# New order of steps, with spent buffers reused, in a fused local-attention and shift-MLP kernel

## The chip, the cores and the metric

The kernel runs on one core of one Trainium2 chip. The metric is the device time of one execution in microseconds (us), as the median of several runs. Engines are named as in the profile: PE (matmul) with PEld (its weight loads), DVE (VectorE), ACT (ScalarE), POOL (GpSimd) and SP (SyncE, which issues most DMAs). "Span" is the time from the first to the last instruction of the profiled execution.

## The reference

One sequence of 2048 rows and 512 columns, bfloat16. Cut to what is computed:

```python
xn  = layernorm(x)
# A: local dilated attention, 32 heads of 16, window 8, dilation 2
q, k, v = split(xn @ wqkv)                  # 512 x 1536
logits[s, u] = q[s] . k[s - 2u] / 4         # u = 0..7, masked where s - 2u < 0
s_out = (sum over u of softmax(logits)[s, u] * v[s - 2u]) @ wo
# B: two-stage MLP
h  = gelu(layernorm(xn) @ w1)               # 512 x 512
hs = concat(h group 0 moved by +1 row, 1 by -1, 2 by +2, 3 by -2) @ w2
x1 = xn + hs
y  = x1 + gelu(layernorm(x1) @ w3) @ w4     # 512 x 1376, 1376 x 512
out = x + s_out * silu(y)
```

## The kernel before

**Tiles and chunks.** The 2048 rows are 4 chunks of 512, and each chunk is 4 tiles of 128 rows; tile i of 0 to 15 lies in chunk i // 4. Rows of a chunk are dealt out so that tile j of it holds rows j, j + 4, j + 8 and so on, which turns the row shifts of B into another tile, or the same tile one column further.

**The order is a list.** All steps are small functions, and the text `ORDER` at the head of the file is a list of tokens such as `w1.3.4`: step `w1` for tile 3 into PSUM bank 4. The program calls them in that order, so each engine gets its own instructions in the order of the list and waits, in order, for what an instruction needs. Nothing reorders them later. A buffer that is asked for again waits until every instruction on the tile that held it has ended.

**The steps, and the engine of each.** SP: `ldx`, `ldxp`, `ldxc` load x; `ldv`, `ldw1`, `ldqk`, `ldw2`, `ldw3`, `ldw4`, `ldwo` load weights; `xT`, `hTr`, `x1Tr`, `oTr`, `tE` are DMA transposes from SBUF to SBUF; `vl.q.i.h` fetches half h of the shifted v rows of tile i from a DRAM copy of v; `pre` copies x into the output, `so` writes a finished tile. DVE: `st` (statistics of x), `nm0` and `nmv` (normalise), `rp`, `rr`, `nb` (small), `pw.c.u` (the product q * k for chunk c and window place u), `smx`, `sms`, `smn` (softmax), `xa` (adds w2's result), `st3s`, `nm3` (second layernorm), `ya` (adds w4's result), `vp` (v times attention), `sg` (gate times wo's result), `fav` (adds x). ACT: `sq0` (root for the first four tiles), `ev0a`, `eqk`, `ev`, `eh`, `eg`, `eo`, `eoT` (copies or GELUs out of PSUM), `nm`, `ex` (exp), `si` (silu). POOL: constants, `rs` and `r3` (powers), `kh` (halo of k), `sv` (stores v to DRAM), `soa` (adds a finished tile into the output by DMA).

**PE work.** `tr0` transposes the first four tiles on PE; the other chunks are transposed by `xT`. `qk` (8 blocks a chunk), `v`, `w1`, `w2` are blocks of 4 matmuls of 128x128 by 512 columns; `w3` also 4 (11 blocks a chunk), `w4` 11 (one block a tile). `lg` (16 small matmuls that sum the products per head), `ws` (8) and `wo` (16) use 32 columns of the array each, at four positions. `oTp` transposes the last two tiles of attention output. Six PSUM banks, 0 to 5, are named by the last number of a token; two more hold the logits.

**Buffers the change touches.** x of chunk 0 has four buffers `x_t` of its own; chunks 1 to 3 take turns in two chunk buffers, `xc0` and `xc1`. Products `pw` take turns in three buffers, the v rows `vs` in three. `wqk_sb` holds the q and k weights, `hT` the turned h, `xnT0` and `xnT1` the turned normalised x of even and odd chunks.

**Waits on SP.** SP issues its DMAs in list order. Each one counts on one of eight semaphores in turn, and a DMA waits for the one eight places ahead of it to have landed.

Of the kernel before, what the change touches and what calls it, by code (L numbers as in the profile page):

```python
# [28 lines left out]
rs.5 w1.6.4 eqk.1.6 sv.7 pw.0.7 lg.0.3 nm.8 w2.0.1 eh.6 xT.4 pw.0.6 w2.1.3 xa.0 lg.0.7 kh.2
lg.0.6 qk.1.3.4 nb.5 rr.5 nm.11 st3s.0 pre.s.0 qk.1.1.1 nm.10 smx.0 eqk.1.3 w1.7.0 xT.5 eqk.1.1  # L30
qk.1.0.4 eh.7 w2.2.1 hTr.3 eqk.1.0 xa.1 ex.0 w2.3.0 pw.1.2 xT.6 v.8.3 pw.1.0 w1.8.4 ev.8 sms.0
lg.1.0 eh.8 sv.8 lg.1.2 w1.9.3 v.9.2 eh.9 pw.1.3 qk.2.6.4 ev.9 hTr.4 qk.2.4.3 sv.9 smn.0 eqk.2.6
qk.2.0.2 eqk.2.4 st3s.1 tE.0 w1.12.4 eqk.2.0 xa.2 rq.0 v.11.3 vl.s.1.1 xa.3 r3.0 eh.12 st3s.2
lg.1.3 ev.11 w2.6.0 nm3.0 nm3.1 sv.11 st3s.3 w2.7.3 x1Tr.0 xa.6 w2.4.4 rq.1 xa.7 ldwo.s.2 r3.1
w2.5.0 st3s.6 xa.4 w1.11.3 st3s.7 qk.2.3.4 eh.11 st3s.4 qk.2.7.1 eqk.2.3 rq.3 nm3.3 r3.3 nm3.2
qk.2.1.3 eqk.2.7 vp.1 w1.10.4 eqk.2.1 vl.s.2.1 x1Tr.1 qk.2.2.1 eh.10 xa.5 ws.1.3 eqk.2.2 st.14
v.10.4 eo.1 vl.s.4.0 st3s.5 hTr.5 qk.2.5.3 ev.10 rp.7 rq.2 pw.1.5 r3.2 w1.13.1 eqk.2.5 vl.s.0.1
sv.10 v.13.4 nm3.7 eh.13 nm3.6 rs.7 nm3.5 w3.0.9.3 x1Tr.3 nm3.4 pw.1.6 w3.0.0.1 eg.0.9 hTr.6
w3.0.3.0 nb.7 rr.7 eg.0.0 pw.1.1 nm.15 w3.0.10.3 x1Tr.2 nm.14 w3.0.4.1 vp.0 eg.0.10 xT.7
w3.0.7.2 eg.0.4 ev.13 w2.9.3 vl.s.2.0 eg.0.3 sv.13 eg.0.7 lg.1.1 xa.9 w2.10.0 pw.1.4 ws.0.3  # L40
lg.1.5 st3s.9 eo.0 vl.s.3.1 lg.1.4 lg.1.6 w3.1.1.2 pw.2.0 v.14.3 vl.s.4.1 pw.2.1 eg.1.1 oTr.0
w1.15.4 ev.14 pw.1.7 qk.3.5.2 sv.14 eh.15 vp.2 qk.3.0.3 kh.3 eqk.3.5 qk.3.2.4 eqk.3.0 qk.3.4.2
eqk.3.2 xa.10 lg.1.7 eqk.3.4 st3s.10 ws.2.0 w3.1.0.4 smx.1 eo.2 qk.3.3.0 eg.1.0 qk.3.1.2 eqk.3.3
ldw4.s.0 pw.2.2 ex.1 w1.14.4 qk.3.6.0 vl.s.3.0 qk.3.7.3 eh.14 sms.1 lg.2.0 lg.2.2 lg.2.1 w2.11.1
eqk.3.1 w2.8.5 eqk.3.6 xa.11 eqk.3.7 w3.0.8.2 vl.s.5.1 xa.8 w3.0.6.3 hTr.7 vp.3 eg.0.8 w3.0.5.5
eg.0.6 w3.0.1.2 eg.0.5 pw.2.3 ws.3.3 eg.0.1 v.12.5 eo.3 pw.2.5 oTr.1 w2.14.3 ev.12 pw.2.4
w2.13.2 sv.12 st3s.8 w2.15.5 xa.13 lg.2.5 lg.2.3 rq.4 smn.1 lg.2.4 r3.4 w2.12.2 pw.3.0 w3.0.2.1
v.15.0 xa.12 vl.s.5.0 eg.0.2 st3s.13 tE.1 w4.3.1 ev.15 pw.2.7 sv.15 vl.s.6.0 nm3.8 nm3.9 st3s.11
w4.2.0 x1Tr.4 ya.3 rq.5 vp.4 si.3 r3.5 w4.0.1 ya.2 nm3.11 si.2 nm3.10 ws.4.0 pw.2.6 w4.1.2 eo.4
vl.s.6.1 ya.0 x1Tr.5 st3s.12 si.0 xa.14 vl.s.7.1 lg.2.6 rq.6 ya.1 w3.1.6.3 r3.6 st3s.14 si.1  # L50
w3.1.2.2 nm3.12 eg.1.6 nm3.13 w3.1.8.1 pw.3.1 w3.2.1.0 eg.1.2 xa.15 eg.1.8 w3.1.7.3 vp.6 eg.2.1
w3.1.5.1 eg.1.7 w3.1.3.0 eg.1.5 st3s.15 w3.1.9.3 eg.1.3 vp.5 vl.s.7.0 w3.1.10.1 eg.1.9 ldwo.s.0
pre.s.2 w3.1.4.0 eg.1.10 rq.7 lg.2.7 eg.1.4 x1Tr.6 r3.7 ws.5.1 pw.3.2 ws.6.3 eo.5 w4.5.0 eo.6
oTr.2 vp.7 vl.s.8.0 vl.s.8.1 w4.4.3 nm3.15 ya.5 smx.2 si.5 w4.7.0 nm3.14 ex.2 ya.4 x1Tr.7 ws.7.3
ya.7 wo.0.1 vl.s.10.0 eo.7 vl.s.10.1 wo.1.0 sms.2 si.4 wo.2.3 wo.3.5 si.7 sg.2 lg.3.0 oTr.3
lg.3.1 lg.3.2 pw.3.3 w3.2.0.2 soa.2 pw.3.5 w4.6.3 eg.2.0 pw.3.4 sg.1 w3.2.3.2 ya.6 soa.1
w3.2.6.0 eg.2.3 sg.0 si.6 sg.3 w3.2.4.3 smn.2 soa.3 w3.3.1.5 soa.0 eg.2.4 w3.2.2.1 vl.s.9.0 tE.2
lg.3.4 lg.3.5 pw.3.7 wo.6.2 eg.3.1 eg.2.2 wo.7.3 sg.6 eg.2.6 lg.3.7 soa.6 sg.7 wo.5.2 soa.7
wo.4.3 sg.5 lg.3.3 soa.5 sg.4 w3.2.5.2 vp.10 soa.4 w3.2.7.3 eg.2.5 w3.2.9.0 eg.2.7 w3.2.10.2
pw.3.6 eg.2.9 ws.10.3 eg.2.10 vl.s.9.1 vp.8 lg.3.6 eo.10 w3.2.8.0 vl.s.13.0 w3.3.0.3 eg.2.8  # L60
smx.3 w4.10.0 eg.3.0 vp.9 w4.8.3 ex.3 ya.10 ws.8.2 sms.3 si.10 ws.9.0 vl.s.13.1 w4.9.1 vl.s.11.0
eo.8 ya.8 eo.9 smn.3 w4.11.0 si.8 vl.s.11.1 ya.9 tE.3 si.9 w3.3.9.1 vl.s.12.0 ya.11 w3.3.5.3
eg.3.9 vp.11 w3.3.4.0 vl.s.12.1 oTr.4 w3.3.6.2 eg.3.4 eg.3.5 w3.3.2.1 vp.13 eg.3.6 ws.11.3
eg.3.2 w3.3.3.2 eo.11 si.11 oTr.5 w3.3.8.3 vp.12 ws.13.1 vl.s.14.1 w3.3.7.0 eg.3.8 vl.s.14.0
# [9 lines left out]
def kernel(  # L74
# [260 lines left out]
    def tr0(i, b):  # L335
        tr_t[i] = bank(b, (P, ND, P), BF16)
        for dt in range(ND):
            nc.tensor.transpose(tr_t[i][:, dt, :], xr[i][:, dt * P : (dt + 1) * P], ident[:])
# [166 lines left out]

    @step
    def pw(c, u):
        pw_t[c, u] = rot("pw", c * W + u, NPW, [P, ND, CH])
        nc.vector.tensor_tensor(  # L509
            out=pw_t[c, u], in0=q_t[c], in1=k_t[c][:, :, DIL * u : DIL * u + CH], op=ALU.mult  # L510
        )
# [243 lines left out]
    def sg(i):  # L755
        nc.vector.tensor_tensor(out=xr[i], in0=mm.pop(("wo", i)), in1=xr[i], op=ALU.mult)  # L756

    @step
    def fav(i):
        nc.vector.tensor_tensor(out=xr[i], in0=xtile(i), in1=xr[i], op=ALU.add)  # L760
# [51 lines left out]
```

## Time and profile before

| what | value |
|---|---|
| median of 3 runs | 198.08 us (197.52 to 199.4) |
| profiled execution, its own time | 197.93 us |
| its span | 195.9 us, 4036 instructions |
| granted TensorE clock | 1.000 |
| DMA moved | 39.53 MB, mean 202 GB/s |
| `pw` x32 on DVE | 37.9 us, 1216 ns each |
| `vp` x16 on DVE | 36.5 us, 2285 ns each |
| `sg` x16 on DVE, out of PSUM | 10.8 us, 687 ns each |
| `fav` x4 on DVE | 1.6 us, 416 ns each |
| `eo` x16 on ACT (a copy out of PSUM) | 9.2 us, 597 ns each |
| loads of ACT's function tables, x20 | 1283 ns each |

A group's mean duration includes the tail of an instruction, under which the next one already starts: in a full queue `pw` follows `pw` after 1.14 us, not 1.22. The row of an `x512` matmul says 379 ns, but in a full queue four of them take 0.86 us. The profiled execution's own time is 2.0 us longer than its span.

### The profile page before, as it was taken

Reading aid. Unit: us, or ns where it says so; the run is one execution under the profiler, and the core shown is the slowest. Engines: PE = TensorE matmul, PEld = TensorE weight load, DVE = VectorE, ACT = ScalarE, POOL = GpSimd, SP = SyncE. Lnnn points to the kernel's source line nnn. Section 1 sums busy time; section 2 is a strip of 40 time slices with the busy share of each in tenths; the row PEclk is TensorE's granted clock in tenths of the full one; section 3 lists DMA queues with packets and bytes.
Section 4 is the critical chain, followed back from the end, with each engine's and each line's share of the span. In section 5 each row is a group of like instructions: output and inputs, shape, how many; then the busy total and the mean of one; then the engine's idle time right before and its main releaser. Section 6 shows DMA issues by size and latency. Waiting matters only on the chain.

```text
span 195.9 us, 4036 instructions
## 1 busy us (share of the span) xinstructions
PE 185.9 (95%) x1590; PEld 84.8 (43%) x1610; DVE 165.3 (84%) x268; ACT 121.5 (62%) x187; POOL 45.7 (23%) x70
## 2 busy tenths in 40 slices
...
GB/s 151 301 351 240 282 360 303 305 225 107 159 182 168 249 138 287 268 347 59 30 222 211 150 333 0 187 204 261 162 214 107 216 144 204 218 298 247 46 27 107
DMA packets 49042, 39.53 MB, mean 202 GB/s; under 512 B 36322, under 2 KB 43344, under 8 KB 48976
## 3 DMA queue, kind: packets, MB, share of 16 engines
...
q0 software_dynamic: 2528, 3.69, 10.0%
...
## 4 chain that ended last, share of the span: by engine, by line
PE 69%; DVE 19%; DMA 6%; issue 2%; SPq 1%; ACT 0%; DVEq 0%
PE mm L664 19%; PE mm L647 18%; PE mm L421 9%; PE mm L747 6%; DVE pw L509 5%; PE mm L707 4%; DMA hT<-ht 3%; PE mm L449 3%; PE mm L474 3%; PE mm L590 3%; PE lg L520 3%; DMA x<-in_A_x_dram 3%; DVE st L315 2%; DVE xr L597 2%; DVE st L601 2%
## 5 line engine op out<-in xcount | busy, mean ns | idle before, releaser
L509 DVE TENSOR_TENSOR pw<-qT,kT 128x2048 bf16<-128x2048 bf16 x32 | 37.9, 1216 | 5.4 <-ACT kT L430 3.0
L647 PE MATMUL mm<-x1T,w_sb 128*128 128x512 bf16 (+1 forms) x176 | 40.2, 379 | 0.0
L664 PE MATMUL mm<-w_sb,h 128*128 128x512 bf16 (+1 forms) x169 | 38.9, 379 | 0.5 <-issue 0.2
L695 DVE TENSOR_TENSOR vs<-vs,att 128x4096 bf16<-128x4096 bf16 x16 | 36.5, 2285 | 2.5 <-DMA vs<-v_dram 2.5
L656 ACT ACTIVATE h<-mm 128x512 bf16<-128x512 f32 (+1 forms) x44 | 24.9, 599 | 18.4 <-PE mm L647 18.2
L421 PE MATMUL mm<-xnT,wqk_sb 128*128 128x512 bf16 x128 | 29.6, 379 | 0.1
L664 PEld LDWEIGHTS <-h 128*128 128x128 bf16 (+1 forms) x176 | 16.7, 98 | 21.5 <-issue 2.1
L647 PEld LDWEIGHTS <-w_sb 128*128 128x128 bf16 (+1 forms) x176 | 17.0, 100 | 20.3 <-issue 1.3
L772 POOL DMA_DIRECT2D out_dram<-xr x12 | 10.5, 913 | 54.3 <-DVE xr L756 54.0
...
L675 ACT ACTIVATE xr<-xr 128x512 bf16<-128x512 bf16 x16 | 10.0, 628 | 16.9 <-DVE xr L671 16.9
L421 PEld LDWEIGHTS <-wqk_sb 128*128 128x128 bf16 x128 | 12.4, 98 | 15.1 <-issue 0.3
L449 PE MATMUL mm<-wv_sb,xnT 128*128 128x512 bf16 x63 | 16.3, 380 | 0.3 <-ACT xnT L346 0.2
L590 PE MATMUL mm<-w_sb,hT 128*128 128x512 bf16 x60 | 15.0, 380 | 1.2 <-DMA hT<-ht 0.9
L474 PE MATMUL mm<-w_sb,xnT 128*128 128x512 bf16 x56 | 15.7, 380 | 0.4
L614 POOL TENSOR_TENSOR rstd<-ve,mhalf 128x2 f32<-128x2 f32 x8 | 9.6, 1205 | 27.0 <-DVE ve L607 27.0
L485 ACT ACTIVATE ht<-mm,rs 128x512 bf16<-128x512 f32 x16 | 11.0, 687 | 7.1 <-PE mm L474 7.1
L747 PE MATMUL mm<-wo_sb,oT 128*32 128x512 bf16 x256 | 15.1, 379 | 0.0
L756 DVE TENSOR_TENSOR xr<-mm,xr 128x512 bf16<-128x512 f32 x16 | 10.8, 687 | 4.5 <-PE mm L747 4.4
L671 DVE TENSOR_TENSOR xr<-mm,xr 128x512 bf16<-128x512 f32 x16 | 10.9, 679 | 4.4 <-PE mm L664 4.4
L720 ACT ACTIVATE o<-mm 128x512 bf16<-128x512 f32 x16 | 9.2, 597 | 6.2 <-PE mm L707 5.9
L520 PEld LDWEIGHTS <-e_log 128*32 128x32 bf16 x512 | 8.5, 96 | 7.9 <-issue 5.9
...
## 6 DMA issues: line engine op xcount, KB each, us to landing
...
```

The lines of the kernel that those rows point to most:

```text
L421: nc.tensor.matmul(pt, lhsT=wqk_sb[:, dt, nt * P : (nt + 1) * P], rhs=xnT[c][:, :, dt, :], start=(dt == 0), stop=(dt == ND - 1),)
L449: nc.tensor.matmul(pt, lhsT=xnT[c][:, jj, dt, :], rhs=wv_sb[:, dt, :], start=(dt == 0), stop=(dt == ND - 1),)
L474: nc.tensor.matmul(pt, lhsT=xnT[c][:, jj, dt, :], rhs=w1_sb[:, dt, :], start=(dt == 0), stop=(dt == ND - 1),)
L485: nc.scalar.activation(ht[i // 2][:, i % 2, :], mm.pop(("w1", i)), AF.Gelu_apprx_tanh, scale=rstd2(i))
L509: nc.vector.tensor_tensor(out=pw_t[c, u], in0=q_t[c], in1=k_t[c][:, :, DIL * u : DIL * u + CH], op=ALU.mult)
L520: nc.tensor.matmul(lg_t[c][32 * jj : 32 * jj + 32, u, :], lhsT=e_log[:, dt, :], rhs=pwt[:, dt, jj * P : (jj + 1) * P], start=(dt == 0), st ...
L590: nc.tensor.matmul(pt, lhsT=hT[:, plane, g, p0 : p0 + P], rhs=w2_sb[:, g, :], start=(g == 0), stop=(g == ND - 1),)
L647: nc.tensor.matmul(pt[:fs, :], lhsT=w3_sb[:, dt, ft * P : ft * P + fs], rhs=x1T[c][:, :, dt, :], start=(dt == 0), stop=(dt == ND - 1),)
L656: nc.scalar.activation(h3[c, ft][:fs, :], mm.pop(("w3", c, ft))[:fs, :], AF.Gelu_apprx_tanh)
L664: nc.tensor.matmul(pt, lhsT=h3[c, ft][:fs, jj * P : (jj + 1) * P], rhs=w4_sb[:fs, ft, :], start=(ft == 0), stop=(ft == NF - 1),)
L695: nc.vector.tensor_tensor(out=vv, in0=vv, in1=att[c][:, :, H * jj : H * jj + H].unsqueeze(2).to_broadcast([P, NB * 2, DH, H]), op=ALU.mult,)
L747: nc.tensor.matmul(pt[T32 * jj : T32 * jj + T32, :], lhsT=oT[2 * c + jj // 2][:, jj % 2, dt, T32 * r : T32 * r + T32], rhs=wo_sb[:, dt, :] ...
```

## The change

Buffers: x of chunk 0 now lies in `xc0`, and the four `x_t` are gone. The products have four buffers, and from product number 8 (the first of chunk 1) also `xc0`, from number 24 (chunk 3) also `xnT0`. The v rows have three buffers, from tile 8 also `wqk_sb` and from tile 13 also `hT`. Which one a product or tile gets is fixed by its number: the one used longest ago.

Steps: tiles 12, 13 and 14 of the last chunk take wo's result out of PSUM on ACT (`ge`) and multiply it on DVE in SBUF (`gb`) in place of `sg`. Tile 15 is done in two halves of 256 columns: `woh` on PE, `sgh` and `favh` on DVE, `soh` on SP. The list of steps is new from the first line on; the PE work in it is the same, and 28 stretches of steps at four array positions (`lg`, `ws`, `wo`) between full blocks are now 27.

```diff
 ORDER = """
-ldx.s.0 c_warm c_small ldv.s.0 kh.0 warmup.10.512.0 sqw ldx.s.1 c_ident ldv.s.1 ldx.s.2 ldw1.s.0
-st.0 c_elog ldx.s.3 sq0.0 ldw1.s.1 nm0.0 ldxp.s.2 st.1 ldxp.s.3 tr0.0.1 ldqk.s.0 warmup.8.128.0
-rp.0 ev0a.0 ldqk.s.1 sq0.1 v.0.1 st.2 ldw4.s.2 rs.0 nm0.1 ldw4.s.1 sq0.2 ev.0 nm0.2 tr0.1.0
-ldwo.s.1 sv.0 rr.0 ev0a.1 st.3 tr0.2.1 ldw2.s w1.0.2 c_zero ev0a.2 rp.1 sq0.3 st.4 ldwo.s.3
-v.1.0 eh.0 nm0.3 w1.1.1 st.7 tr0.3.3 st.6 rs.1 w1.2.4 ev.1 st.5 ev0a.3 sv.1 v.2.0 eh.1 rp.3 rp.2
-rr.1 rs.2 qk.0.2.3 hTr.0 ev.2 eh.2 qk.0.5.1 sv.2 rr.2 nmv.5 eqk.0.2 c_sel nmv.4 qk.0.3.4 eqk.0.5
-xT.2 qk.0.7.3 rs.3 eqk.0.3 qk.0.1.1 ldxc.s.2 eqk.0.7 nmv.7 nmv.6 qk.0.6.4 rr.3 eqk.0.1 ldxc.s.3
-xT.3 qk.0.0.3 eqk.0.6 qk.0.4.1 eqk.0.0 ldw3.s.1 pre.s.1 w1.3.4 eqk.0.4 v.3.3 pw.0.0 kh.1 eh.3
-w1.4.1 ev.3 pw.0.2 ldw3.s.0 v.5.4 sv.3 hTr.1 eh.4 pw.0.1 lg.0.2 ev.5 v.4.1 pw.0.5 sv.5 lg.0.0
...
-w4.14.3 soa.11 eoT.14 wo.13.5 ya.14 si.14 wo.14.3 sg.13 wo.15.4 fav.13 sg.14 so.s.13 wo.12.5
-sg.15 fav.14 sg.12 so.s.14 fav.15 fav.12 so.s.15 so.s.12
+ldx.s.0 c_warm c_small ldv.s.0 kh.0 warmup.10.512.0 sqw ldx.s.1 c_ident ldv.s.1 ldx.s.2 st.0
+c_elog sq0.0 ldw1.s.0 nm0.0 ldx.s.3 st.1 ldw1.s.1 tr0.0.1 ldxp.s.3 warmup.8.128.0 ev0a.0 rp.0
+ldxp.s.2 sq0.1 v.0.1 ldqk.s.0 nm0.1 ldqk.s.1 c_sel st.2 ldwo.s.3 tr0.1.0 ldw3.s.1 ev0a.1 st.3
+c_zero ev.0 v.1.0 sq0.2 rp.1 sq0.3 nm0.2 w1.0.1 ldwo.s.0 ev.1 nm0.3 tr0.2.2 st.5 tr0.3.0 rs.1
+w1.1.3 ldwo.s.1 ev0a.3 st.6 ldw4.s.2 rs.0 ev0a.2 w1.3.0 ldw2.s rr.1 st.4 ldxc.s.2 sv.0 qk.0.0.2
+eh.3 rr.0 st.7 sv.1 qk.0.2.4 rp.2 rp.3 rs.2 qk.0.7.5 eh.0 rs.3 qk.0.6.0 nmv.4 eh.1 nmv.5 eqk.0.0
+rr.2 hTr.0 qk.0.5.3 nmv.6 eqk.0.6 rr.3 nmv.7 v.3.2 eqk.0.5 xT.2 eqk.0.7 v.2.0 ev.3 w1.2.5
+ldxc.s.3 sv.3 ev.2 xT.3 eqk.0.2 qk.0.3.2 sv.2 eh.2 st.11 qk.0.4.4 eqk.0.3 hTr.1 st.8 qk.0.1.5
+eqk.0.4 st.10 kh.1 eqk.0.1 st.9 w1.4.4 vl.s.0.0 pw.0.0 ldw4.s.1 v.4.5 eh.4 vl.s.2.0 rp.5 v.5.2
+rp.4 ev.4 rs.5 st.15 w1.5.4 ev.5 st.13 sv.4 qk.1.2.5 rs.4 eh.5 rr.5 nb.5 st.14 nm.11 qk.1.5.2
+hTr.2 sv.5 st.12 eqk.1.2 qk.1.7.4 eqk.1.5 rp.7 vl.s.1.1 rp.6 rs.7 qk.1.4.5 nb.4 rr.4 eqk.1.7
+pw.0.2 nm.9 w2.1.2 rs.6 nm.8 rr.7 lg.0.2 nb.7 xa.1 w2.0.4 nm.14 xT.4 pw.0.6 nm.15 v.7.2 eqk.1.4
+pre.s.2 st3s.1 v.6.0 ev.7 nb.6 rr.6 w1.6.5 sv.7 nm.12 xa.0 ldw4.s.0 pw.0.1 w1.7.2 eh.6 w2.2.4
+st3s.0 eh.7 ev.6 lg.0.1 pw.0.3 hTr.3 w2.3.2 nm.13 sv.6 nm.10 xa.2 lg.0.6 lg.0.3 xa.3 w1.9.0
+pw.0.7 v.8.2 pre.s.0 eh.9 xT.5 st3s.2 v.9.4 ev.8 st3s.3 w1.8.0 sv.8 ev.9 rq.0 pw.0.5 r3.0 lg.0.7
+eh.8 lg.0.0 qk.1.6.4 sv.9 rq.1 nm3.1 vl.s.2.1 r3.1 nm3.0 lg.0.5 eqk.1.6 pw.0.4 qk.1.3.0 x1Tr.0
+w2.4.4 nm3.2 kh.2 eqk.1.3 nm3.3 lg.0.4 x1Tr.1 xa.4 w2.5.0 smx.0 qk.1.1.4 vl.s.1.0 qk.1.0.2
+eqk.1.1 qk.2.3.5 eqk.1.0 xT.6 xa.5 ex.0 qk.2.0.4 pw.1.3 xT.7 qk.2.6.0 pw.1.2 qk.2.1.2 hTr.4
+eqk.2.0 lg.1.3 sms.0 eqk.2.6 lg.1.2 v.11.4 eqk.2.3 vl.s.0.1 eqk.2.1 v.10.5 ev.11 qk.2.2.2 sv.11
...
+pw.2.0 w2.12.4 eqk.3.4 st3s.4 qk.3.5.0 xa.12 ldw3.s.0 qk.3.3.5 st3s.7 eqk.3.5 ldwo.s.2 qk.3.2.4
+st3s.5 eqk.3.3 qk.3.1.0 rq.3 st3s.10 eqk.3.2 r3.3 lg.1.5 rq.2 st3s.12 eqk.3.1 vl.s.8.1 r3.2
...
+eg.1.6 x1Tr.5 w3.1.7.0 w2.13.1 vl.s.9.0 eg.1.7 lg.2.7 xa.13 vl.s.13.0 lg.2.5 eg.1.1 lg.2.6
+lg.2.3 pw.3.5 vl.s.13.1 eg.1.10 ws.4.1 ws.3.3 eo.4 w4.5.2 st3s.13 eo.3 si.3 pw.3.4 oTr.1 nm3.14
+oTr.2 rq.6 smx.2 w4.4.3 r3.6 vl.s.7.0 vl.s.6.0 vl.s.6.1 w4.7.1 ya.5 ex.2 vl.s.7.1 nm3.13 pw.3.1
...
+oTp.14.2 eoT.15 w4.14.3 soa.10 eoT.14 woh.15.0.2 ya.14 woh.15.1.1 sgh.15.0 si.14 wo.13.3
+sgh.15.1 favh.15.0 favh.15.1 wo.14.1 soh.s.15.0 ge.13 soh.s.15.1 wo.12.2 gb.13 ge.14 fav.13
+gb.14 so.s.13 ge.12 fav.14 gb.12 so.s.14 fav.12 so.s.12
 """
...
-    NPW, NVS, NH3, NVT, NHT, NOT = 3, 3, 13, 3, 2, 3
+    NPW, NVS, NH3, NVT, NHT, NOT = 4, 3, 13, 3, 2, 3
...
+    def tags(first, more):
+
+        out = []
+        use = list(first)
+        last = {t: -1 for t in use}
+        for k in range(max(NT, NCH * W)):
+            for t in more.get(k, ()):
+                use.append(t)
+                last[t] = -1
+            t = min(use, key=lambda t: (last[t], use.index(t)))
+            last[t] = k
+            out.append(t)
+        return out
+
+    pw_tag = tags([f"pw{k}" for k in range(NPW)], {W: ["xc0"], 3 * W: ["xnT0"]})
+    vs_tag = tags([f"vs{k}" for k in range(NVS)], {8: ["wqk_sb"], 13: ["hT"]})
...
-    x_t = [fixed(f"x{i}", [P, D]) for i in range(TPC)]
...
-        return x_t[i] if i < TPC else x_c[i // TPC][:, i % TPC, :]
+        return x_c[i // TPC][:, i % TPC, :]
...
-        pw_t[c, u] = rot("pw", c * W + u, NPW, [P, ND, CH])
+        pw_t[c, u] = sb.tile([P, ND, CH], BF16, name="pw", tag=pw_tag[c * W + u])
...
-            vs[i] = rot("vs", i, NVS, [P, 2, NB, D])
+            vs[i] = sb.tile([P, 2, NB, D], BF16, name="vs", tag=vs_tag[i])
...
+    def ge(i):
+        tg[i] = rot("vt", i, NVT, [P, D])
+        nc.scalar.activation(tg[i], mm.pop(("wo", i)), AF.Copy)
...
+    def gb(i):
+        nc.vector.tensor_tensor(out=xr[i], in0=tg.pop(i), in1=xr[i], op=ALU.mult)
...
+    def woh(i, h, b):
+        pt = mm["wo", i, h] = bank(b)
+        c, r = i // TPC, i % TPC
+        for dt in range(ND):
+            for jj in range(TPC):
+                nc.tensor.matmul(
+                    pt[T32 * jj : T32 * jj + T32, 0:DH2],
+                    lhsT=oT[2 * c + jj // 2][:, jj % 2, dt, T32 * r : T32 * r + T32],
+                    rhs=wo_sb[:, dt, h * DH2 : (h + 1) * DH2],
+                    start=(dt == 0), stop=(dt == ND - 1), tile_position=(0, T32 * jj),
+                )
...
+    def sgh(i, h):
+        x = xr[i][:, h * DH2 : (h + 1) * DH2]
+        nc.vector.tensor_tensor(out=x, in0=mm.pop(("wo", i, h))[:, 0:DH2], in1=x, op=ALU.mult)
...
+    def favh(i, h):
+        x = xr[i][:, h * DH2 : (h + 1) * DH2]
+        nc.vector.tensor_tensor(
+            out=x, in0=xtile(i)[:, h * DH2 : (h + 1) * DH2], in1=x, op=ALU.add
+        )
...
+    def soh(q, i, h):
+        qs[q].dma_start(
+            out=rows(out2, i)[:, h * DH2 : (h + 1) * DH2], in_=xr[i][:, h * DH2 : (h + 1) * DH2]
+        )
```

More of the change, by code (lines that the diff above doesn't have):

```diff
@@ L29 @@
[L29 to L64, printed above, removed]
@@ new lines @@
+pw.1.7 ev.10 qk.2.7.4 sv.10 eqk.2.2 smn.0 v.13.5 eqk.2.7 pw.1.0 w1.12.2 tE.0 v.14.4 pw.1.1 eh.12
+w2.7.0 pw.1.4 w2.6.3 ev.13 xa.7 lg.1.7 ev.14 sv.13 lg.1.1 xa.6 lg.1.0 w1.13.0 sv.14 pw.1.6
+lg.1.4 eh.13 qk.2.5.3 st3s.6 hTr.6 vp.1 lg.1.6 eqk.2.5 qk.2.4.0 w1.11.3 eqk.2.4 vp.0 w1.10.4
+eh.11 ws.1.0 eh.10 v.12.3 eo.1 hTr.5 pw.2.3 w1.15.0 ev.12 vl.s.4.1 pw.2.1 w1.14.4 sv.12 ws.0.3
+vp.2 v.15.5 eo.0 eh.15 w2.10.3 eh.14 vl.s.4.0 w2.8.0 pw.1.5 ev.15 hTr.7 ws.2.4 sv.15 xa.10
+qk.3.7.5 kh.3 eo.2 xa.8 oTr.0 qk.3.0.4 pw.2.4 eqk.3.7 qk.3.6.0 eqk.3.0 st3s.8 qk.3.4.5 eqk.3.6
```

42 lines of the change are left out of this document (32 added, 10 removed).

## The prediction

> **What bounds the kernel now.** First the page: busy time, and the chain that ended last.
>
> ```profile
> PE 185.9 (95%) x1590; PEld 84.8 (43%) x1610; DVE 165.3 (84%) x268; ACT 121.5 (62%) x187; POOL 45.7 (23%) x70
> ...
> PE 69%; DVE 19%; DMA 6%; issue 2%; SPq 1%; ACT 0%; DVEq 0%
> ```
>
> PE is busy in nearly all of the span, and DVE is not far behind, so the question is how much of PE's time is work. In a full queue four 512-column matmuls follow in 0.863 us, 0.2158 each. From the first qk block (its weight load starts at 14.14) the list holds 648 full matmuls = 139.8; 16 wo at 0.863 = 13.8; 16 ws at 0.43 = 6.9; 32 lg at 0.2225 = 7.1; two oTp = 0.45. Going over to four array positions and back costs too: v.5's weights start at 23.64 and lg.0.2's at 24.80, 1.17 for a 0.86 block, and lg.0.2 takes 0.37 for 0.22; single stretches come out 0.22 to 0.26 over their work, so 28 at 0.24 = 6.7. Sum 174.85, which from 14.14 gives 189.0. wo.12, the last block, starts at 190.39 and so ends at 191.25. PE thus stands still for only 2.3 us after the start. The view of PE's waits names them, with the one at the start:
>
> ```profile
> PE mm L338 <- DVE xr L327: 1.5, 1, 1.5
> ...
> PE mm L590 <- DMA hT<-ht: 0.9, 1, 0.9
> PE lg L520 <- DVE pw L509: 0.4, 1, 0.4
> ```
>
> Columns: total us, times, longest. So there is little to win: the start, those 2.3 us, and what follows PE's end. The chain in order of time shows the start, and the timeline shows the end:
>
> ```profile
> 2.64 4.92 DMA x<-in_A_x_dram
> 7.59 0.71 DVE st L315
> ...
> 8.59 0.41 DVE xr L327
> ...
> 9.58 0.40 PE mm L338 x4
> ```
>
> ```profile
> 188.01 3.64 PE L747 MATMUL mm<-wo_sb,oT 128*32 128x512 bf16 x64
> ...
> 190.24 1.28 DVE L756 TENSOR_TENSOR xr<-mm,xr 128x512 bf16<-128x512 f32 x2
> ...
> 191.44 0.41 DVE L760 TENSOR_TENSOR xr<-xc,xr 128x512 bf16<-128x512 bf16 x1
> 191.77 0.68 DVE L756 TENSOR_TENSOR xr<-mm,xr 128x512 bf16<-128x512 f32 x1
> 192.37 0.75 DVE L760 TENSOR_TENSOR xr<-xc,xr 128x512 bf16<-128x512 bf16 x2
> ```
>
> At the start DVE stands at st.2 until x's third tile lands at 7.59; nm0.1, whose data was there at 5.9, is queued behind it, and PE waits for it from 7.4 to 9.05. At the end, sg.12, then fav.15 and fav.12, then a store.
>
> **Start.** nm0.1 goes ahead of st.2. It needs sq0.1, which ended at 6.68: 0.13 + 0.41, done at 7.25, before x's third tile. tr0.1 follows v.0 at 7.4, ev0a.1 runs 7.85 to 8.45 (the row's 0.43 from tr0 to its copy), then v.1 to 9.4, w1.0 to 10.2 (w1's second half landed at 9.30). st.2 ends at 8.46, st.3 at 9.5 (x's fourth tile landed at 8.66), nm0.2 at 10.05, nm0.3 at 10.55; tr0.2, tr0.3, w1.1 and w1.3 end at 12.7, and ev0a.2 at 12.2. So qk starts at 12.7 with five blocks done, where before six were done at 14.14, five at 13.28: **-0.6 us**. The first half of wqk landed at 12.23 and the second at 13.98; it is first needed at 14.4, by qk.0.7: free.
>
> **Stretches.** 28 become 27: -0.24. The pure sum is 12.7 + 0.86 + 174.85 - 0.24 = 188.2, against 189.0.
>
> **Loads moved on SP.** Here I see the price. In the trace every SP transfer lands in the order of issue. The transpose xT.2, which w1.4 and v.4 need, was issued at 16.9; the view of its line in that window ends so:
>
> ```profile
> L402 SPq DMA_TRANSPOSE xnT<-xr x1: 2667/2667/2667, 16.9 to 16.9; - x1
> ...
> DMA to landing us min/median/max: 5.0/5.0/5.0
> ```
>
> It landed at 21.9, 0.9 before w1.4 at 22.77. Between wqk (13.98) and hTr.0, the queue held w4 (640 and 96 KB), two wo parts and w2: 1504 KB. In the new list it holds one half of w3 (688 KB), three wo parts, w4's 96 KB, w2, and x of chunk 2 (512 KB), which went after xT.2 before: 2192 KB, 688 KB more. The rows put a price on it from both sides. By what the engines moved from 14 to 18 us, 298 GB/s, 0.70 MB are 2.35 us: xT.2 at 24.2. By single landings (1504 KB in 5.8 us for 1 KB rows, the same half of w3 in 2.1 us, x of chunk 3 in 1.4) it comes at 23.3. I take the middle, 23.7, as the queue is a mixture of these. In the new list eleven blocks follow 12.7, so PE asks for w1.4 at 22.2 and **stands 1.45 us** (1.0 to 2.0). Nothing else is queued on PE that could run: in order, w1.4, v.4, v.5 and w1.5 all need it. On ACT eh.4 and ev.4 wait with it.
>
> DVE meets the same queue: st.11, st.8, st.10, st.9 (0.81 each) now stand ahead of pw.0.0 and need x of chunk 2, at 21.3 to 22; pw.0.0 starts at about 24.8 where it started at 22.09. DVE does not lose by it, as the old list did these four after pw.0.5: 22.09 + 3.2 = 25.3.
>
> **Middle.** I added up DVE's queue from pw.0.0 = 24.8 (pw 1.14, st and st3s 0.82, xa 0.60, vp 2.20, smx 2.4, sms 2.48, nm3 0.33) and PE's from 12.7, and compared them where one needs the other. DVE is late by 1.2 at lg.0.2, 1.1 at v.7 and v.8 (banks freed by xa.1 and xa.3), 0.9 at qk.2.6 and lg.1.2, under 0.7 at all later places. PE's wait of 1.45 covers these, but xa.4 then waits for w2.4, and places come back where two engines wait for each other in turn: qk.2.6 for xa.5, lg.1.2 for pw.1.2, w1.15, w2.10 and qk.3.0 each 0.2 for an eo on ACT. The old list has 2.3 - 0.9 = 1.4 us of that kind. I take **1.2 us** (0.3 to 2.3). The 0.9 for hT goes: the transpose that came late had a v fetch and two transposes queued ahead of it, and here hTr.5 has only hTr.6 and lands some 0.7 before w2.10 asks.
>
> **Buffers.** More product buffers spare DVE waits for PE: in the page's groups 2.2 us before pw. They lie after 119 us, where DVE's sums are 3 to 10 us ahead of PE's: 0. New waits on SP: vl.8.1 waits for the last qk block in the list, and behind it stand vl.3.1, vl.3.0, x1Tr.3 and x1Tr.2; tile 3's product is due 14 us later, and nm3.6 some 9: 0. ldxc.2 waits for nm0.3 (10.55), and is issued at about 12.8, when the nine loads ahead of it are: 0. vl.13.0 waits for w2.13, behind it oTr.1, whose eo.3 comes later anyway: 0. If a cover fails, a late v fetch costs its median 5.0 us from issue less the cover.
>
> **End.** PE's sum is equal (two half blocks of 0.43 for one of 0.86). wo.12's result goes through ge (0.60), gb and fav (0.33 each in a full queue) and not sg (0.60) and two favs (0.33 each), as fav.15 is gone from between; sg.12 also began 0.15 late, behind fav.14. So **-0.1 us**, and a store after it as before (1.8 to landing). [...]
>
> **Sum.** PE's end: 188.2 + 1.45 + 1.2 = 190.85 against 191.25, -0.4; with the end -0.5. The profiled execution took 197.93 (its span of 195.93 and 2.0 around it): 197.4; it lies 0.15 under the median, 198.08, so **197.6 us** for the median.
>
> **Rivals.** (a) *The transposes come in time.* If the added loads run at the 351 GB/s that the page's third slice shows, ahead of need, xT.2 lands by 22.3 and PE does not wait: -1.45, so 196.1; with the waits in turn at their lower bound 195.2. For it: 0.70 MB is only 2 us at that rate, and engines idle in part until 6 us. Against it: DMA is at 9 tenths from the second slice on, so nothing is free. [...]
>
> (b) *The queue stays late (slower than before).* Behind xT.2 come x of chunk 3, xT.3, hTr.1, a v fetch, w4's 640 KB, another v fetch, and only then hTr.2, which w2.2 needs. From rows (1.4, 1.0, 0.9, 1.9, 2.7, 1.9, 1.0) it lands 10.8 us after xT.2, at 34.5, and PE asks at 36.2. If they run as the trace's window from 18 to 22 us did, 211 GB/s, and not as the next one, 277, that is 14.2 us, landing at 37.9, and with xT.2 at its late end at 38.4: PE stands another 1.7 to 2.2, and hTr.3 and xT.4 lie behind. 197.6 + 1.7 = 199.3, with 0.5 for xT.2 and 0.7 for what lies behind 200.5. It decides when hTr.2 lands after 36.2. For it: the old hTr.2 took 6.0 us from issue to landing; against it: it was not waited for.
>
> (c) *The change doesn't do what it says:* the buffers bring nothing, as PE never waited for a buffer, and the early nm0.1 only moves the wait to w1.4. That is nearly the forecast; without my waits in turn growing, 198.0, no change.
>
> **How the numbers follow.** Forecast 0.52, (a) 0.24, (b) 0.15, (c) 0.09. The range of the forecast alone takes xT.2's +-0.5 and the waits' -0.9 and +1.1: 196.3 to 199.0. Two in ten left out: down to 195.6 (half of (a)'s case below its 196.1) and up to 199.9 (the lower part of (b)). One per cent is 2 us, about what a measurement here can tell from none: below 196.1 lies most of (a) = 0.22; above 200.06 part of (b) and a tail of the forecast = 0.13; the rest 0.65.
>
> **What would show it.** The first qk block near 12.7; PE waiting at w1.4, released by the transposed x, about 1.45; pw.0.0 near 24.8; no wait of w2 for hT in the waits of PE; PE's end near 190.9 in the profile; 27 stretches. Wrong if w1.4 starts without a wait ((a)), if w2.2 waits for hT ((b)), or if a v fetch or x1T shows among PE's releasers.

## The result and the profile after

| | kernel before | changed kernel |
|---|---|---|
| median | 197.89 us (6 runs, 197.52 to 199.4) | 205.37 us (6 runs, 204.25 to 207.61) |
| profiled execution, its own time | 197.93 us | 204.25 us |
| its span | 195.9 us | 202.3 us |
| granted TensorE clock | 1.000 | 0.986 |

The ratio is 1.0369, with a 95% interval of 1.0313 to 1.0426: slower, where the forecast was no change. (Medians count every run except one disturbed one of 496.04 us in an experiment below; the ratios also leave out runs that lie over 1.5% above the fastest of their kernel.)

The page of the changed kernel: busy time of the engines, the granted clock in 40 slices, the chain that ended last.

```profile
PE 188.7 (93%) x1626; PEld 85.1 (42%) x1626; DVE 165.0 (82%) x270; ACT 122.6 (61%) x190; POOL 41.3 (20%) x70
...
PEclk9999969999999999999999999999999999999997
...
PE 57%; DMA 15%; issue 13%; DVE 9%; POOL 2%; SPq 1%; ACT 1%; POOLq 0%; ACTq 0%
```

PE has the same work and is busy 2.8 us longer (188.7 against 185.9) in a span that is 6.4 us longer. One slice in the middle of PE's work shows a clock of 6 tenths (the 7 of the last slice stands where PE is done), and DMA holds 15% of the chain in place of 6%. The view of PE's waits of the changed kernel (total us, times, longest) says for what it stood:

```profile
PE mm L492 <- DMA xnT<-xr: 4.1, 1, 4.1
PE mm L439 <- ACT vt L477: 1.4, 2, 0.8
...
PE mm L665 <- DMA x1T<-xn: 0.6, 1, 0.6
PE mm L765 <- issue: 0.6, 1, 0.6
```

The first is w1.4 waiting for xT.2 (L492 is `w1`), as forecast, but three times as long. Taken from start to start it is 4.45 us: PE's work ends at 22.24, and w1.4 starts at 26.69. The view of the transposes' line in the window in which xT.2 is issued has its landing 8.1 us after that, against 5.0 before:

```profile
L420 SPq DMA_TRANSPOSE xnT<-xr x1: 3505/3505/3505, 18.6 to 18.6; - x1
...
DMA to landing us min/median/max: 8.1/8.1/8.1
```

Stretches of one us of the changed kernel, each with its length and the busy time of PE, PEld, DVE, ACT and POOL, then the granted clock, the share of the 16 DMA engines, and GB/s:

```profile
23.00:24.00 1.00, 0.00 (x0) 0.00 (x0) 0.93 (x5) 0.25 (x1) 0.00 (x0) 1.00 2.24 226
24.00:25.00 1.00, 0.00 (x0) 0.00 (x0) 0.97 (x4) 0.00 (x0) 0.00 (x0) 1.00 0.28 18
25.00:26.00 1.00, 0.00 (x0) 0.00 (x0) 0.96 (x3) 0.00 (x0) 0.00 (x0) 0.98 0.78 272
26.00:27.00 1.00, 0.30 (x1) 0.13 (x2) 1.00 (x5) 0.00 (x0) 0.00 (x0) 0.50 0.99 369
...
29.00:30.00 1.00, 1.00 (x6) 0.40 (x4) 0.93 (x6) 0.50 (x2) 0.00 (x0) 0.82 0.97 264
```

Two things are to be seen. From 24 to 25 us the engines moved 18 GB/s although xT.2 was in flight and two transfers were queued behind it: the packets that had begun at about 23.4 all ended together at 25.3 to 25.4 (the share of 2.24 a row above is packets booked in the us of their start). And from 25.95 to 29.37 us the granted clock is 0.50, so the matmuls of w1.4 and v.4 followed each other after 0.43 us, where they follow after 0.22: 0.39 and 0.70 us more by the starts of their weight loads, 1.1 together.

PE's end moved from 191.25 to 197.28, by 6.03. The sum over all blocks of PE's list, each from start to start less its work, gives that: the first qk block starts 0.7 earlier (12.57 with five blocks done, against 13.28), and from there PE loses 15.74 us where it lost 9.02. Some 6.6 us of both sums are the going over to four array positions and back. Of the rest of the 15.74, 4.45 are at w1.4 and 1.1 the clock, 0.57 at qk.0.7 for the second half of wqk, 0.96 at qk.1.6, 0.46 at qk.3.7, 0.94 in wo.3 and 0.96 around w3.3.2. What follows PE's end to the last landing is 3.71 us, against 3.78.

### The profile page after: what moved, and what is told of

Same layout as the page of the kernel before. It is cut to its first block, busy times and chain, and to the rows that moved or that the text cites. A ratio compares the mean times of both kernels' runs of the same rounds, so it can differ in the third digit from the quotient of the medians.

```text
span 202.3 us, 4090 instructions
## 1 busy us (share of the span) xinstructions
PE 188.7 (93%) x1626; PEld 85.1 (42%) x1626; DVE 165.0 (82%) x270; ACT 122.6 (61%) x190; POOL 41.3 (20%) x70
## 4 chain that ended last, share of the span: by engine, by line
PE 57%; DMA 15%; issue 13%; DVE 9%; POOL 2%; SPq 1%; ACT 1%; POOLq 0%; ACTq 0%
PE mm L665 15%; PE mm L682 13%; PE mm L439 6%; PE mm L765 6%; PE mm L608 4%; DVE vs L713 4%; DMA wqk_sb<-in_A_wqkv_dram 4%; DMA xnT<-xr 4%; PE mm L492 3%; PE lg L538 3%; PE mm L467 3%; DMA x1T<-xn 2%; DMA v_dram<-vt 2%; PE mm L725 2%; DMA wv_sb<-in_A_wqkv_dram 2%
## 5 line engine op out<-in xcount | busy, mean ns | idle before, releaser
L682 PE MATMUL mm<-w_sb,h 128*128 128x512 bf16 (+1 forms) x176 | 39.4, 379 | 0.0
L492 PE MATMUL mm<-w_sb,xnT 128*128 128x512 bf16 x64 | 16.7, 395 | 4.1 <-DMA xnT<-xr 4.1
L337 DVE BATCH_NORM_STATS2 st<-xc 128x6 f32<-128x512 bf16 x16 | 10.8, 678 | 8.3 <-DMA xc<-in_A_x_dram 8.3
L608 PE MATMUL mm<-w_sb,hT 128*128 128x512 bf16 x64 | 16.0, 380 | 0.0
L632 POOL TENSOR_TENSOR rstd<-ve,mhalf 128x2 f32<-128x2 f32 x8 | 7.3, 912 | 42.2 <-DVE ve L625 42.0
L765 PE MATMUL mm<-wo_sb,oT 128*32 128x512 bf16 x240 | 14.2, 379 | 0.6 <-issue 0.6
L477 ACT ACTIVATE vt<-mm 128x512 bf16<-128x512 f32 x16 | 9.4, 596 | 5.6 <-PE lg L538 1.8
```

Source lines behind the costliest of these rows:

```text
L337: nc.vector.bn_stats(out=st1[:, i, :], in_=xtile(i))
L492: nc.tensor.matmul(pt, lhsT=xnT[c][:, jj, dt, :], rhs=w1_sb[:, dt, :], start=(dt == 0), stop=(dt == ND - 1),)
L608: nc.tensor.matmul(pt, lhsT=hT[:, plane, g, p0 : p0 + P], rhs=w2_sb[:, g, :], start=(g == 0), stop=(g == ND - 1),)
L682: nc.tensor.matmul(pt, lhsT=h3[c, ft][:fs, jj * P : (jj + 1) * P], rhs=w4_sb[:fs, ft, :], start=(ft == 0), stop=(ft == NF - 1),)
L765: nc.tensor.matmul(pt[T32 * jj : T32 * jj + T32, :], lhsT=oT[2 * c + jj // 2][:, jj % 2, dt, T32 * r : T32 * r + T32], rhs=wo_sb[:, dt, :] ...
```

## The experiments

Some diffs of the list do not show the line that a moved step leaves; each moved step stands in the list once.

The theory: the time went into the first 30 us, where the change puts 688 KB more ahead of xT.2 on SP, and into a few waits behind it that the new list brings of itself. The rivals: it is the new order of the whole list, or the buffers, or something at 23 to 25 us that has nothing to do with what was put ahead.

**The loads put back, in two steps.** The first moves w3's second half behind xT.3:

```diff
-ldwo.s.3 tr0.1.0 ldw3.s.1 ev0a.1
+ldwo.s.3 tr0.1.0 ev0a.1
...
-xT.3 eqk.0.2
+xT.3 ldw3.s.1 eqk.0.2
```

> The changed kernel with one step moved: the load of w3's second half (688 KB) goes behind xT.3 on SP, where it stood before the change; x of chunk 2 and all else stay. Theory (the bytes ahead of xT.2 in SP's queue set its landing): w3's half took 3.1 us in the queue (15.31 to 18.41), so xT.2 lands near 23.5 instead of 26.65, PE stands about 1.3 us at w1.4 instead of 4.45, too short for the halved clock; 205.4 - 3.1 - 1.1 = 201.2 us. Rival (what holds xT.2 is the stall of 23.1 to 25.4 us, in which the 4 KB store packets of v took 1.9 us each, and not the queue ahead): xT.2 still lands after 25.4, PE stands 3 us or more, 204 to 205.4 us.

Measured: 199.41 us (10 runs, 198.38 to 202.56), ratio to before 1.0076 (1.0046 to 1.0106). xT.2 landed at 23.18, PE lost 0.89 us at w1.4, and the clock stayed at 1. The theory's landing is right within 0.3. The time fell by 6.0 and not 4.2; one part of the difference is that PE, arriving at another moment, no longer waited at qk.1.6. The second step also moves x of chunk 2 behind xT.2, as before the change, and its four `st` behind pw.0.0 on DVE:

```diff
-ldw2.s rr.1 st.4 ldxc.s.2 sv.0
+ldw2.s rr.1 st.4 sv.0
...
-xT.2 eqk.0.7
+xT.2 ldxc.s.2 eqk.0.7
...
-pw.0.0 ldw4.s.1
+pw.0.0 st.11 st.8 st.10 st.9 ldw4.s.1
```

> As the run with w3's half behind xT.3, and x of chunk 2 goes behind xT.2 too, where it stood before the change, with its four st behind pw.0.0 on DVE: the bytes ahead of xT.2 are then fewer than before the change. Theory (bytes ahead of xT.2): xT.2 lands by 22.3, PE does not wait at w1.4, no halved clock, pw.0.0 starts near 22.5: 205.4 - 4.45 - 1.1 = 199.8 us (199.0 to 200.6); what is left over the 197.9 of before are the waits of the changed list behind it. Rival (the stall at 23.1 to 25.4): 203.5 us or more.

Measured: 202.51 us (4 runs, 201.61 to 203.35), ratio 1.023 (1.0179 to 1.0282). xT.2 landed at 20.68 and w1.4 did not wait at all, as the theory has it, but the time is 2.7 us above its 199.8. The waits of PE in this run:

```profile
PE mm L439 <- DMA xnT<-xr: 2.3, 1, 2.3
```

Line 439 is `qk`: the next transpose, xT.3, behind the two x loads, landed at 28.33, where the run above had 26.63, and qk.1.2 stood for it. The clock was halved again, from 29.0 to 32.4, for another 1.6 us. So the queue as a whole is late, and what is taken from ahead of one transpose stands ahead of the next.

**The same loads in the kernel before.** Only SP's order is changed there:

```diff
-ldqk.s.1 sq0.1
+ldqk.s.1 ldw3.s.1 sq0.1
...
-ldwo.s.3
+ldwo.s.3 ldxc.s.2
...
-hTr.1 eh.4
+hTr.1 ldw4.s.1 eh.4
```

> The kernel before with only SP's loads in the changed order: w3's second half directly behind the second half of wqk, x of chunk 2 ahead of hTr.0, 640 KB of w4 behind hTr.1. Nothing else of the change. Theory (the order of the loads alone costs the time): xT.2 lands near 26, PE stands at w1.4 for 3 to 4 us and the clock is halved after it: 197.9 + 3 to 5 = 201 to 203 us. Rival (the loads are hidden, and the time was lost in the rest of the list or the shared buffers): 197.5 to 198.5 us.

Measured: 200.85 us (4 runs, 200.21 to 201.67), ratio 1.0149 (1.0106 to 1.0193). xT.2 landed at 25.21, PE lost 2.85 at w1.4, the clock stayed at 1.00 from 22 to 32 us. The order of the loads alone makes the old kernel slower by some 3 us, just under the low end of what was expected.

**The gap filled.** Sixteen matmuls that compute nothing stand ahead of w1.4:

```diff
-st.9 w1.4.4
+st.9 warmup.16.512.3 w1.4.4
```

> The changed kernel with 16 idle matmuls of 512 columns (16 x 0.2158 = 3.45 us) ahead of w1.4 on PE, which compute nothing that is used; the loads stay. Theory (the granted clock of one half from 25.95 to 29.37 us comes from PE standing still for over 3 us): the clock is 1.0 to the end of PE's work, w1.4 and v.4 get their 1.1 us back, xT.2 lands where it did and w1.4 starts near 26.7: 205.4 - 1.1 = 204.3 us. Rival (the clock falls for another reason): the dip stays and the time is 205.4 us.

Measured: 200.84 us (4 runs, 200.09 to 201.16). The stretches of this run, columns as above:

```profile
24.00:25.00 1.00, 1.00 (x6) 0.43 (x5) 0.96 (x3) 0.00 (x0) 0.00 (x0) 1.00 0.43 48
...
26.00:27.00 1.00, 0.26 (x2) 0.00 (x0) 1.00 (x2) 0.00 (x0) 0.00 (x0) 1.00 0.95 362
27.00:28.00 1.00, 0.63 (x3) 0.31 (x4) 0.57 (x5) 0.00 (x0) 0.48 (x1) 1.00 1.19 313
```

The clock is 1.00 in every stretch from 22 to 30 us, so its fall did come from PE standing still; and the DMA engines stand still at 24 us as before (48 GB/s), with xT.2 landing at 27.32, 3.62 behind hTr.0 (3.44 in the changed kernel). But the time fell by 4.5 us by the medians, and by 3.1 between the two profiled executions, where the clock explains 1.1. What else changed in the trace is that the waits in wo.3 and at w3.3.2 were gone and those at qk.1.6 and qk.3.7 smaller, which no theory had expected.

**The instruction stream moved.** Those 16 matmuls are 32 instructions with their weight loads, so all that follows on PE stands 32 places later. The next run moves it without touching the gap, from the run with w3's half behind:

```diff
-warmup.10.512.0 sqw
+warmup.10.512.0 warmup.16.8.0 sqw
```

> The run with w3's half behind xT.3, and 16 idle matmuls of 8 columns more at the start, while PE has nothing else to do; they move every later instruction of PE on by 32 places in its stream. In the changed kernel and in both runs with moved loads PE waits 0.6 to 1.0 us at lg.3.7 with nothing that releases it ('issue'), and 0.9 to 1.1 us at w3.3.2 for the last x1T; in the run with 16 idle matmuls in the gap at w1.4 both are gone. Theory (they hang on where the fetches of 16 KB of instructions fall): both are gone here, 199.4 - 1.6 = 197.8 us. Rival (they hang on when the steps come, later or earlier, and not on the stream): both stay, 199.4 us.

Measured: 200.12 us (10 runs, 198.78 to 203.11): no gain. Both waits were gone; but PE lost 2.8 us at qk.1.6 and 1.1 at w2.4 instead. Most of the 1.1 is the clock, which is one half from 45.97 to 49.38, after that stop. The timeline of ACT shows what qk.1.6 stood for; the bracket is idle time and what ended it:

```profile
40.05 0.60 ACT L477 ACTIVATE vt<-mm 128x512 bf16<-128x512 f32 x1
44.31 0.60 ACT L477 ACTIVATE vt<-mm 128x512 bf16<-128x512 f32 x1 [3.67 <-DMA v_dram<-vt]
```

ev.9 needs the buffer from which the store of tile 6 reads. That store was issued at 36.90, and its packets ended at 43.4: the DMA engines stood still once more, from 40.5 to 42.2. The new list has ev.9 close behind ev.6, with three `vt` buffers.

The wait within wo.3 is shown by the timeline of PE: here in the changed kernel,

```profile
138.02 1.89 PE L765 MATMUL mm<-wo_sb,oT 128*32 128x512 bf16 x29
140.47 0.40 PE L765 MATMUL mm<-wo_sb,oT 128*32 128x512 bf16 x3 [0.56 <-issue]
```

and here in the run with the shifted stream, where the 32 matmuls of wo.2 and wo.3 follow without a break:

```profile
136.19 1.93 PE L765 MATMUL mm<-wo_sb,oT 128*32 128x512 bf16 x32
```

In the five traces of the changed list without the shift wo.3 took 1.50 to 2.25 us from its first weight load to its last; in the five with it 0.66 to 0.69, one of which had a break of 0.2 in lg.3.7 instead. In each of the first five a 16 KB instruction fetch begins 0.3 to 0.8 us ahead of wo.3 (at 138.06, taking 1.01 us, in the changed kernel), in the others 2.4 to 2.8 ahead. So this wait does hang on the place in the stream. That the fetch makes it is inferred from these times, and a fetch alone is not enough: in the four traces of the old list one begins 0.8 to 1.1 us ahead of wo.3 too, which takes 0.66 there. The wait at w3.3.2 does not hang on the stream alone: of the five traces with the shift, it is gone or nearly so in three, and came back in the two with four `vt` buffers below.

**More room ahead of the transposes.** To the run with w3's half behind, two edits: the three parts of wo go behind it too, and qk.0.7 changes places with v.3.

```diff
-ldqk.s.1 c_sel st.2 ldwo.s.3
+ldqk.s.1 c_sel st.2
...
-qk.0.7.5 eh.0
+v.3.5 eh.0
...
-v.3.2 eqk.0.5 xT.2 eqk.0.7 v.2.0 ev.3
+qk.0.7.2 eqk.0.5 xT.2 ev.3 v.2.0 eqk.0.7
...
-xT.3 ldw3.s.1
+xT.3 ldw3.s.1 ldwo.s.3 ldwo.s.0 ldwo.s.1
```

> The run with w3's half behind xT.3, and two edits more: the three parts of wo that still stood ahead of xT.2 go behind w3's half, and qk.0.7 changes places with v.3 on PE (and their copies on ACT), so that PE does not ask for the second half of wqk at 14.0 but 0.86 later. Theory (bytes ahead of xT.2 set its landing; their landings were 0.6 us apart each): xT.2 lands near 21.7 and not 23.18, so the 0.9 us at w1.4 go; the 0.8 us at qk.0.7 (released at 14.76 by wqk) go too: 199.4 - 1.7 = 197.7 us. Rival (a transpose's own time differs from one to the next and sets the landing, not the bytes): xT.2 or xT.3 comes as late as before and PE waits at w1.4 or at qk.1.2, 199 us or more.

Measured: 201.82 us (4 runs, 200.23 to 202.25): the rival. xT.2 landed at 20.82 and neither w1.4 nor qk.0.7 waited, but the waits came back behind them:

```profile
PE mm L608 <- DMA hT<-ht: 1.0, 1, 1.0
...
PE mm L439 <- DMA xnT<-xr: 0.8, 1, 0.8
```

xT.3 landed 2.69 behind the load ahead of it, and hTr.1 at 31.54 behind wo's parts, where it had been 29.24; w2.1 (L608) waited for it. All three edits together:

> The edits of the two runs above together (w3's half and the three parts of wo behind xT.3, qk.0.7 and v.3 exchanged, 16 small idle matmuls at the start). If both theories hold: 199.4 - 1.7 - 1.6 = 196.1 us, faster than the kernel before (197.7). If only the loads' theory holds 197.7, if neither 199.4.

Measured: 202.03 us (4 runs, 201.41 to 202.83). By the profile PE lost 2.3 us at w2.1 for hTr.1 and 2.5 at qk.1.6 for the store.

**The start alone**, in the kernel before:

```diff
-v.0.1 st.2 ldw4.s.2 rs.0 nm0.1
+v.0.1 nm0.1 st.2 ldw4.s.2 rs.0
```

> The kernel before with one step moved: nm0.1 ahead of st.2 on DVE, as in the change. Theory (the start's part of the change is worth what the changed kernel's trace shows, its first qk block with five blocks done at 12.57 against 13.28): PE's wait of 1.5 us for the normalised second tile is cut, 197.7 - 0.6 = 197.1 us (196.8 to 197.4). Rival (w1's second half, which landed at 9.30, takes over the wait, as w1.0 follows tr0.1 in this list): 197.7 us.

Measured: 197.84 us (10 runs, 197.27 to 198.88), ratio 0.998 (0.9951 to 1.0009). The rival, with another releaser: tr0.1 ran at 7.06 in place of 9.05, but in this list tr0.2 follows it and needs nm0.2, so PE waited for DVE 2.2 us in one piece, and the first qk block came at 14.27, where it had been 14.14. The edit needs the rest of the new start to be of use. xT.2, with the same transfers ahead of it as in the kernel before, landed at 24.24 in this run and not at 21.88, and cost PE 1.4 us at w1.4. In the run with the value buffers alone, further below, which has the same transfers ahead of it too, it landed at 24.19.

**Four buffers for the values on their way to the store.** To the run with w3's half behind and the shifted stream:

```diff
-    NPW, NVS, NH3, NVT, NHT, NOT = 4, 3, 13, 3, 2, 3
+    NPW, NVS, NH3, NVT, NHT, NOT = 4, 3, 13, 4, 2, 3
...
-    warm = fixed("warm", [P, CH])
+    warm = sb.tile([P, 2, NB, D], BF16, name="warm", tag="vs2")[:, 0, 0, :]
```

> The run with w3's half behind xT.3 and 16 small idle matmuls at the start, with four buffers in place of three for the copied values on their way to the store of v (the room comes from the constant zeros of the start, which share a buffer of the value products). There PE waited 2.8 us at qk.1.6 and 1.1 at w2.4, behind ACT's ev.9, which stood 3.67 us for the store of tile 6 to leave its buffer. Theory (three buffers are too few where the stores take 6.5 us to land): both waits go, 200.1 - 3.2 = 196.9 us, and the runs lie closer together. Rival (behind that wait another stands that comes as late): 199 to 200 us.

Measured: 197.08 us (10 runs, 195.95 to 198.95), ratio to before 0.9926 (0.9888 to 0.9964): as expected, and faster than both kernels. Its page and its waits:

```profile
PE 186.9 (96%) x1642; PEld 85.1 (44%) x1642; DVE 164.2 (84%) x270; ACT 122.7 (63%) x190; POOL 39.5 (20%) x70
```

```profile
PE mm L492 <- DMA xnT<-xr: 1.3, 1, 1.3
...
PE mm L665 <- DMA x1T<-xn: 0.3, 1, 0.3
```

No wait for ACT's `vt` is left, and w1.4 costs 1.7 us from start to start. The new list and the shared buffers are all in this kernel, so neither as a whole made the changed kernel slow, only what these three edits mend. The same two edits, with the loads as the change has them:

> The changed kernel with its loads where the change put them, with the four buffers and the 16 small idle matmuls of the run above; the two differ in the place of w3's half alone. Theory: PE still stands about 4.4 us at w1.4 and the clock is halved after it (5.5 us together); what the buffers and the shifted stream take off are the 1.6 us at qk.1.6 and qk.3.7 and the 1.6 at lg.3.7 and w3.3.2: 205.4 - 3.2 = 202.2 us, some 5 above the run with w3's half behind. Rival (the later waits are only the late start carried on): 204 to 205.4 us.

Measured: 201.92 us (3 runs, 200.09 to 202.31), ratio 1.0133 (1.0047 to 1.0218). Its waits:

```profile
PE mm L492 <- DMA xnT<-xr: 3.2, 1, 3.2
...
PE mm L665 <- DMA x1T<-xn: 0.6, 1, 0.6
```

This pair is the plainest statement of the price: two kernels that differ in the place of one load of 688 KB are 4.8 us apart by these medians, 4.1 by the ratios.

**The stores of v out of the way.** The packets that stood for 1.9 us in the changed kernel were those stores':

```diff
-ldxc.s.3 sv.3 ev.2 xT.3 eqk.0.2 qk.0.3.2 sv.2 eh.2
+ldxc.s.3 ev.2 xT.3 eqk.0.2 qk.0.3.2 eh.2
...
-kh.1 eqk.0.1
+kh.1 sv.3 sv.2 eqk.0.1
```

> The changed kernel with the stores of v's tiles 3 and 2 behind kh.1 on POOL, so that they are issued 2 to 3 us later (22.7 in place of 19.34 and 20.10) and their packets come when xT.2 has passed. Nothing else. Theory (the stores lengthen the standstill of the DMA engines in xT.2, in which 13 of their 4 KB packets took 1.9 us): xT.2 takes 1.0 to 1.3 us behind hTr.0 (23.21) in place of 3.44, lands near 24.4, PE stands 2.2 us and the clock stays: 205.4 - 2.3 - 1.1 = 202.0 us. Rival (the standstill belongs to the transpose itself, or to the 16 KB instruction fetch at 23.14): xT.2 lands near 26.6 as before, 205.4 us.

Measured: 204.09 us (4 runs, 203.1 to 205.09), ratio 1.0278 (1.0222 to 1.0335), nearer to the rival's 205.4 than to the theory's 202.0. Its stretches:

```profile
23.00:24.00 1.00, 0.00 (x0) 0.00 (x0) 0.81 (x3) 0.38 (x1) 0.90 (x2) 1.00 2.42 236
24.00:25.00 1.00, 0.00 (x0) 0.00 (x0) 0.96 (x4) 0.00 (x0) 0.00 (x0) 1.00 0.06 7
25.00:26.00 1.00, 0.00 (x0) 0.00 (x0) 0.96 (x3) 0.00 (x0) 0.00 (x0) 0.91 1.07 325
```

The stores' packets now ran from 25.6 to 27.5, and still nothing moved at 24 us: the packets that stood were the transposes' own, hTr.0 landed at 25.37 in place of 23.21, and xT.2 at 26.19. The stores were caught in the standstill and did not make it.

**The value buffers alone**, in the kernel before, with its list:

```diff
...
-            vs[i] = rot("vs", i, NVS, [P, 2, NB, D])
+            vs[i] = sb.tile([P, 2, NB, D], BF16, name="vs", tag=vs_tag[i])
```

> The kernel before, its own list, with one part of the change alone: the fetched values use the spent buffers of the q/k weights from tile 8 and of the turned h from tile 13, beside their own three. Theory (the term of the prediction: DVE's waits for buffers lie off PE's path): 197.9 us, no difference. Rival (values that come earlier cut PE's waits at ws, or the earlier fetches press the queue): 0.5 us or more to either side.

Measured: 198.47 us (10 runs, 197.48 to 200.0), ratio 1.0 (0.9969 to 1.003): nothing, as forecast. The product buffers were not tried alone.

## Why the prediction was wrong, by its own steps

The forecast had PE's end at 190.85, and it came at 197.28, 6.4 us later: 3.0 at w1.4, 1.1 by the clock, and 2.4 by other waits, 3.6 in place of the 1.2 forecast (the last five listed with the result, less 0.3 at qk.1.6 for the going over to `lg`). (The upper end of the range adds up to 199.2 and not 199.0; nothing hangs on it.)

- **Start, -0.6:** right (12.57 against the forecast 12.7), but PE then only stands the longer for xT.2. The second half of wqk, called free at 13.98, landed at 14.63, and qk.0.7 lost 0.57 us for it. The gain comes from the whole new order of the start; nm0.1 alone in the old list brings 0.998 (0.9951 to 1.0009).
- **Loads moved on SP, "stands 1.45 us":** this is the step that failed, and by size. PE asked for w1.4 at 22.24, as forecast (22.2), but xT.2 landed at 26.65 in place of 23.7, and PE stood 4.45 us. The added loads were priced right: from the second half of wqk to the last load ahead of hTr.0 the queue took 7.71 us, where the old trace had 5.82; that is 1.89 more, against 1.8 in the forecast. (The half of w3 took 3.1 us, 15.31 to 18.41, and not 2.1; the others took less.) Of the 2.95 us, 0.65 is the later landing of wqk, and 2.2 is the transpose itself: the sum took over its old row, 1.21 behind hTr.0, and here it was 3.44. That row was one draw from a wide spread. Of the transposes in the twelve traces in which every landing on SP is recorded, 239 of 256 KB were issued 2 us or more before the transfer ahead of them landed (those of the attention weights, `tE`, are left out). The time behind the one before has a median of 1.07 us, a tenth of them take 2.3 or more, and the longest 3.75; the kernel before has one of 3.43 itself. So the base of the sum was luck: with the old transfers ahead of it, xT.2 landed at 21.88 in the trace that the forecast used, and at 24.24 and 24.19 in two other runs. Even the forecast's upper bound, 24.2, was below what came.
- **DVE meets the same queue, pw.0.0 at 24.8:** 25.58, and off PE's path as forecast. The timeline of DVE shows the stop for x of chunk 2:

```profile
22.37 0.69 DVE L337 BATCH_NORM_STATS2 st<-xc 128x6 f32<-128x512 bf16 x1 [4.63 <-DMA xc<-in_A_x_dram]
```

- **What a wait of this length brings along** was not in the sum: the halved clock, 1.1 us. The run with the gap filled shows its cause.
- **Stretches, -0.24:** too small to be told here; what PE loses beside the waits is some 6.6 us, where it was 6.7.
- **Waits in turn in the middle, 1.2:** of those named (lg.0.2, v.7, qk.2.6, lg.1.2) none shows in PE's waits. None shows in the run with four `vt` buffers either, in which PE stood at w1.4 about as long as forecast (1.7 us), so PE's lateness is not why. In their place came waits that the forecast did not have: for the second half of wqk at qk.0.7 (0.57), for `vt` at qk.1.6 and qk.3.7 (1.4 in the view), for x1T at w3.3.2 (0.6), in wo.3 (0.6). The forecast named x1T among what would prove it wrong. The run with four `vt` buffers shows the first of them to be a buffer too few behind stores that are late; the new list has ev.9 close behind ev.6, and the prediction did not count the `vt` buffers at all.
- **hT, 0.9 gone:** right, no w2 waits for hT in the changed kernel.
- **Buffers, 0:** right for the values (ratio 1.0). For the products, DVE's wait of 2.2 us before `pw` became 0.0, off PE's path.
- **End, -0.1:** right, 3.71 against 3.78 from PE's end to the last landing.
- **Rival (b), the queue stays late:** its sign was right and its place wrong. hTr.2 did land after 36.2, at 37.20, but PE was so late that it did not wait for it; the loss came three transposes earlier, at xT.2. The run with x of chunk 2 behind too shows that a rival at xT.3 was as possible.
- **Landings in order of issue:** they are, in all twelve of those traces (96 transfers in the kernel before, 97 in the changed one).
